# Casting q and k of a pair in one operation, with the tail weights of a spatial product made earlier

## The chip, the cores and the metric

The kernel runs on one core of one Trainium2 chip: TensorE (PE) for matrix products, VectorE (DVE), ScalarE (ACT) and GpSimd (POOL) for the rest, and SyncE (SP), which here only issues DMAs; POOL issues DMAs too. The metric is the device time of one execution in microseconds (us), and lower is better.

## The reference

A gated attention for 8 batches of 8 heads (sequence 576, head dimension 64), whose output goes through a gated MLP with a spatial product over the sequence:

```python
scores = scale * np.matmul(q, k.transpose(0, 1, 3, 2))
cum = np.cumsum(np.maximum(s, 0.0), axis=-1)
bias = -(cum[:, :, :, None] - cum[:, :, None, :])
scores = np.where(causal, -1e9, scores + np.minimum(bias, 0.0))
attn = softmax(scores)
x = (attn @ v) with the heads put side by side        # (8, 576, 512)
h = np.maximum(x @ w_in, 0.0)                          # (8, 576, 1024)
u, v = h[..., :512], h[..., 512:]
v_n = (v - mean(v)) / sqrt(var(v) + 1e-6)
v_s = np.einsum('ts,bsd->btd', w_spatial, v_n) + b_spatial[None, :, None]
return (u * v_s) @ w_out
```

All of it is float32 outside the kernel; w_in and w_out come as float64 and are taken apart bit by bit.

## The kernel before

Products run in float16 with each operand split in two: a high part (the cast to float16) and a low part (the operand less its high part). Attention is done in 32 pairs of heads, p = 0 to 31; the MLP in 8 batches, one for four pairs.

*Scores.* For pairs 3 to 31 (pairs 0 to 2 use float32 operands directly) the scores of a pair are two products added up in PSUM (L300 to 304): QA with KA, and QB with KB, each of 128 rows that are summed over. KA holds in rows 64 to 127 the high part of k and in rows 61 to 63 the prefix sums of s in three parts (`cc`, brought by `aux_rows`, L212, three DMAs); QA holds in rows 64 to 127 the high part of q and in rows 0 to 63 the constant 8 (131360.0 as a float32 is two float16 8.0), so that rows 61 to 63 add 8 times the prefix sums; rows 0 to 60 of KA are zero. Both are set once by POOL (`init_static`, L130). KB and QB carry the cross terms: low k with high q in the lower half, high k with low q in the upper half. There are three buffers of each, used in turn (p % 3).

*How a pair is split.* `load_raw` (L227, POOL's queue) brings k in partitions 0 to 63 and q in partitions 64 to 127 of one float32 tile. `split_raw` (L233) then does k and q one after the other: DVE casts k to a tile kh of 64 partitions, of which there is one buffer; SP sends it to KA and to KB; DVE makes the low part of k. ACT casts q into QA, SP sends it on to QB, and POOL makes the low part of q in four pieces.

*Softmax and the second product.* `s_pass` (L276): DVE adds the mask and takes the row's extreme (L307), ACT takes the exponential (L313), DVE the reciprocal of the sum (L317, L318), ACT and DVE the high and low part of the weights (L322, L323), and SP transposes them with a DMA (L328), two large ones and one for the last 64 rows per pair. `av_pass` (L401 and L408) multiplies with v, whose two parts `fetch_v` and `load_v` (L255, L263) prepare for two pairs at a time.

*MLP.* For each batch: the v half in five tiles of 128 rows, the last one of 64 rows laid on both halves of the partitions (L443, normalised in L459 to L478: POOL makes 1/sqrt(var), L469 and L470, and six DMAs spread the last tile over vx and VY, L482 to 484); then the u half (L494); then the spatial product (L507), which ends with the last 64 rows: L509 takes vx with wx1, and L510 takes VY with wx2, whose rows 0 to 63 are the low part of the tail weights and whose rows 64 to 66 are the bias in three parts; then the output product (L529).

*Order.* PE's order is written by hand: each step has a position on a common axis (`at`, L545), scores of pair p stand at 2p to 2p + 5/3, the second product at 2p + 3.72, the MLP of batch b from 8b + 10.3 on, and PE follows the sorted list. The other engines and the two DMA queues are ordered by a list planner, by position and by when it reckons things to be ready; steps marked `True` go first, and those before position 12.4 that are not so marked follow the last marked one on their engine. An engine runs its list in order, and a DMA that waits holds up what is behind it on its queue.

*Weights.* While the first pairs run, the kernel also brings and splits its weights: w_in (`fetch_win`, `load_win`), w_spatial (`load_wsp`, L190, positions 11 to 12.2), w_out (`load_wout`, L187, 10.6 to 13.9) and the tail with the bias (`load_wtail`, L195, position 13). The first spatial product stands at about 13.9, the first output product at about 16.1.

Of the kernel before, what the change touches and what calls it, by code (L numbers as in the profile page):

```python
# [19 lines left out]
SWSP = 1024.0  # L20
# [10 lines left out]
def attn_gated_mlp(ctx, tc, kqT, v, s, w_in, w_spT, b_sp, w_out, outT):  # L31
    nc = tc.nc
    P = 128
    NHB, D, H, S = kqT.shape
# [95 lines left out]
    def init_static(i):  # L130

        nc.gpsimd.memset(QA[i][0:64].rearrange("p h s -> p (h s)").bitcast(F32), 131360.0)
        nc.gpsimd.memset(KA[i][0:64].rearrange("p h s -> p (h s)").bitcast(F32), 0.0)
        if i < 2:
            nc.gpsimd.memset(VY[i][64:96], 2048.0)
# [59 lines left out]
    def load_wtail():  # L195
# [3 lines left out]
        split_w(wx1, wx2, s4, SWSP, N_W3 > 4)  # L199
        bf = wk.tile([1, S], F32, tag="ob", bufs=2, name="bf")  # L200
        bp = wk.tile([1, 3, S], F16, tag="wst", bufs=1, name="bp")
        nc.sync.dma_start(out=bf, in_=b_sp)
# [5 lines left out]
        for i in range(3):  # L208
            nc.sync.dma_start(out=wx2[TAIL + i:TAIL + i + 1], in_=bp[:, i])
# [13 lines left out]
    def raw_rows(hb, hs, nm):  # L223
        src = kqT[hb, 0:64, hs] if nm == "k" else kqT[hb, 64:128, hs]
        return nc.sync.dma_start(out=raws[hb, hs.start, nm][64:128], in_=src)

    def load_raw(p):  # L227
# [3 lines left out]
        nc.gpsimd.dma_start(out=raws[p], in_=kqT[hb, :, 2 * pr:2 * pr + 2])  # L231

    def split_raw(nm, p):  # L233


        i = p % 3
        raw = raws[p] if nm == "k" else raws.pop(p)
        lo, hi = slice(0, 64), slice(64, 128)
        if nm == "k":
            kh = wk.tile([64, 2, S], F16, tag="kh", bufs=1, name=f"kh{p}")  # L240
            nc.vector.tensor_copy(kh, raw[lo])
            nc.sync.dma_start(out=KA[i][hi], in_=kh)
            nc.sync.dma_start(out=KB[i][hi], in_=kh)
            nc.vector.tensor_tensor(out=KB[i][lo], in0=raw[lo], in1=kh, op=ALU.subtract)
        else:
            nc.scalar.copy(QA[i][hi], raw[hi])  # L246
            nc.sync.dma_start(out=QB[i][lo], in_=QA[i][hi])
            for j in range(2):
                for c in (slice(0, TH), slice(TH, S)):
                    nc.gpsimd.tensor_tensor(out=QB[i][hi, j, c], in0=raw[hi, j, c], in1=QA[i][hi, j, c],  # L250
                                            op=ALU.subtract)
# [319 lines left out]
    at(-18.9, True, native_cum, 1)  # L571
    at(0.5, True, behind, "c", load_raw, 3)
# [3 lines left out]
    at(1.9, True, aux_rows, 3)  # L576
    for nm in "kq":
        at(2.1, True, split_raw, nm, 3)
# [7 lines left out]
    for hb in range(2, NHB):  # L586
        for pr in range(2):
            p = 2 * hb + pr
            at(2 * p - 5.2, False, load_raw, p)
            at(2 * p - 1.2, False, aux_rows, p)  # L590
# [77 lines left out]
```

## Time and profile before

| | |
|---|---|
| median of 3 runs | 743.84 us (746.62, 743.84, 734.99) |
| the profiled execution | 734.97 us |
| its span, first to last instruction | 733.2 us |
| mean granted clock of PE | 0.943 |
| busy, us | PE 600.2, DVE 607.0, ACT 520.9, POOL 226.0 |
| DMA queue of SP (hardware) | 78.74 MB, 57.2% of 16 engines' span |
| DMA queue of POOL (software) | 35.07 MB, 16.5% |

Busy time is the time in which an engine runs instructions; idle time counts only where it ends on what is late, and the profile names the releaser of each wait. PE is the engine that ends the program. "Granted clock" is the share of TensorE's full speed that the throttle allowed. The page cuts the span in 40 slices of 18.3 us; a digit is the busy share in tenths:

```profile

DVE  8889999795879899789979898999789897985531
PEclk9788577995999999999999999999999999999999
DMA  8997747866279597967797698969986979465001
```

### The profile page before, as it was taken

The numbers are of one execution on the slowest core, as the hardware profiler recorded it, in microseconds if no ns is written. First come the engines' busy times: TensorE is split into PE (matmuls) and PEld (weight loads), VectorE is DVE, ScalarE is ACT, GpSimd is POOL, SyncE is SP. The second block draws the span as 40 slices with busy tenths as digits, with TensorE's granted clock in tenths as the row PEclk, the third lists the DMA queues.
The fourth block names the chain that finished last, engine by engine and source line by source line (L and its number), as shares of the span: only waits on it lengthen the run. The fifth ranks groups of instructions, "written<-read, shape, count | busy, mean of one in ns | idle before, by whom it ended". The sixth has DMA issues, their size and how long they took to land. (4 is left out here: it accounts for less than half of the span.)

```text
span 733.2 us, 15915 instructions
## 1 busy us (share of the span) xinstructions
PE 600.2 (82%) x5696; PEld 415.7 (57%) x5696; DVE 607.0 (83%) x1660; ACT 520.9 (71%) x1328; POOL 226.0 (31%) x303
## 2 busy tenths in 40 slices
PE   4474375741998899889989889997999898999997
PEld 2152132531774677466756666565756665777576
DVE  8889999795879899789979898999789897985531
ACT  4787578663678777877877868786788787875322
POOL 9105465451123432342225331432034322100100
PEclk9788577995999999999999999999999999999999
DMA  8997747866279597967797698969986979465001
GB/s 224 289 201 132 199 99 198 171 176 156 56 169 202 131 180 181 209 136 160 177 191 161 159 163 184 211 128 167 206 200 123 178 131 179 99 107 123 32 13 64
DMA packets 235101, 114.81 MB, mean 157 GB/s; under 512 B 213471, under 2 KB 216717, under 8 KB 235022
## 3 DMA queue, kind: packets, MB, share of 16 engines
q1 hardware_dynamic: 225726, 78.74, 57.2%
q0 software_dynamic: 9296, 35.07, 16.5%
q8 instruction: 44, 0.72, 0.4%
q14 instruction: 35, 0.29, 0.1%
HBM read 37.28 MB, written 9.44 MB: 64 GB/s over the span
## 5 line engine op out<-in xcount | busy, mean ns | idle before, releaser
L313 ACT ACTIVATE p<-psS,mx 128x256 f32<-128x256 f32 (+3 forms) x256 | 132.9, 524 | 72.5 <-DVE mx L307 57.9
L250 POOL TENSOR_TENSOR QB<-raw,QA 64x288 f16<-64x288 f32 x116 | 118.4, 1049 | 213.2 <-ACT QA L246 175.9
L307 DVE CUSTOM_DVE_ANT_0 psS<-psS,mb 128x512 f32<-128x512 f32 (+2 forms) x320 | 154.3, 493 | 14.2 <-PE psS L303 12.0
L323 DVE SCALAR_TENSOR_TENSOR pb<-p,sm,pb 128x384 f16<-128x384 f32 (+3 forms) x256 | 134.8, 559 | 2.1 <-ACT pb L322 1.6
L322 ACT ACTIVATE pb<-p,sm 128x384 f16<-128x384 f32 (+3 forms) x256 | 122.8, 555 | 7.0 <-DVE sm L318 3.2
L443 PE MATMUL vps<-win,xt 128*128 128x512 f16 (+1 forms) x576 | 105.2, 354 | 18.6 <-ACT ob L532 9.6
L303 PE MATMUL psS<-KA,QA 128*128 128x128 f16 (+1 forms) x348 | 82.9, 312 | 40.4 <-ACT p L313 37.7
L507 PE MATMUL sps<-ws,vn 128*128 128x288 f16 x768 | 106.7, 289 | 10.8 <-DVE g L512 7.2
L494 PE MATMUL ups<-xt,win 128*128 128x288 f16 x768 | 106.6, 293 | 0.6 <-ACT u L497 0.4
L529 PE MATMUL ops<-g,wo 128*128 128x288 f16 x768 | 101.8, 286 | 1.1 <-DVE g L515 1.0
L507 PEld LDWEIGHTS <-vn 128*128 128x128 f16 x768 | 74.6, 99 | 35.9 <-issue 13.2
L494 PEld LDWEIGHTS <-win 128*128 128x128 f16 x768 | 75.6, 100 | 28.7 <-issue 5.1
L303 PE MATMUL psS<-KB,QB 128*128 128x128 f16 (+1 forms) x348 | 89.3, 306 | 1.1 <-DMA QB<-QA 1.1
L529 PEld LDWEIGHTS <-wo 128*128 128x128 f16 x768 | 74.5, 98 | 24.3 <-issue 2.0
L443 PEld LDWEIGHTS <-xt 128*128 128x128 f16 (+1 forms) x576 | 48.4, 103 | 67.8 <-issue 29.4
L401 PE MATMUL av<-pT,V 128*64 128x128 f16 (+2 forms) x960 | 64.0, 282 | 19.7 <-DMA pT<-pb 19.6
L401 PEld LDWEIGHTS <-V 128*64 128x64 f16 x960 | 52.0, 114 | 37.2 <-issue 26.6
L469 POOL TENSOR_SCALAR rs<-mv 128x1 f32<-128x1 f32 x40 | 12.5, 312 | 134.1 <-DVE mv L467 124.0
L303 PEld LDWEIGHTS <-QA 128*128 128x128 f16 x348 | 30.6, 103 | 39.1 <-issue 29.1
L313 ACT ACTIVATION_READ_ACCUMULATOR p<-psS,mx 128x1 f32 x256 | 51.0, 199 | 0.0
L514 ACT CAST g<-g 128x288 f16<-128x288 f32 x64 | 27.1, 429 | 30.4 <-DVE g L512 29.1
L303 PEld LDWEIGHTS <-QB 128*128 128x128 f16 x348 | 30.2, 103 | 30.1 <-issue 16.3
(121 smaller groups left out, 923.4 us busy)
## 6 DMA issues: line engine op xcount, KB each, us to landing
raw<-in_kqT_dram POOLq DMA_DIRECT2D x29, 576.0 KB, 4.7
out_dram<-ob SPq DMA_DIRECT2D x32, 288.0 KB
vraw<-in_v_dram POOLq DMA_DIRECT2D x16, 512.0 KB, 6.9
KA<-kh SPq DMA_DIRECT2D x29, 144.0 KB
KB<-kh SPq DMA_DIRECT2D x29, 144.0 KB
QB<-QA SPq DMA_DIRECT2D x29, 144.0 KB
wst<-in_w_in_dram POOLq DMA_DIRECT2D x8, 512.0 KB, 7.4
vraw<-in_v_dram POOLq DMA_DIRECT2D x16, 128.0 KB, 6.9
```

Source lines behind the costliest of these rows:

```text
L250: nc.gpsimd.tensor_tensor(out=QB[i][hi, j, c], in0=raw[hi, j, c], in1=QA[i][hi, j, c], op=ALU.subtract)
L303: nc.tensor.matmul(ps[m, c0:c0 + w], U[i][:, g, q0:q0 + n], T[i][:, g, k0:k0 + w], start=st, stop=not st)
L307: nc.vector.tensor_tensor_reduce(out=ps[:, c0:c0 + w], in0=ps[:, c0:c0 + w], in1=mask, op0=ALU.add, op1=ALU.min, scale=-0.125, scalar=3.0e ...
L313: nc.scalar.activation(p32, ps[:, c0:c0 + w], AF.Exp, bias=mx[:, col:col + 1], scale=-1.0, accum_out=sm[:, acc:acc + 1])
L322: nc.scalar.activation(dst[:, off:off + w], p32, AF.Copy, bias=0.0, scale=sm[:, col:col + 1])
L323: nc.vector.scalar_tensor_tensor(out=dst[:, n + off:n + off + w], in0=p32, scalar=sm[:, col:col + 1], in1=dst[:, off:off + w], op0=ALU.mul ...
L401: nc.tensor.matmul(dst, V[i][:, jc, h + j], rhs, start=jc == n == 0 and q0 > 0, stop=jc == 3 and n == 2)
L443: nc.tensor.matmul(ps[m, 0:w], xx[:, c, t * P:t * P + (m.stop - m.start)], ww[:, c, NF + g * w:NF + g * w + w], start=c == n == 0, stop=c ...
L494: nc.tensor.matmul(ps[:, 0:TH], ww[:, c, fs], xx[:, c, ts], start=n == 0, stop=n == 3 * KC - 1)
L507: nc.tensor.matmul(ps[:, 0:TH], vv[:, c, fs], ww[:, c, ts], start=n == 0, stop=False)
L514: nc.scalar.copy(g1[:, f, ts], g32)
L529: nc.tensor.matmul(ps[:, 0:TH], ww[:, f, ms], gg[:, f, ts], start=n == 0, stop=n == 3 * FC - 1)
```

## The change

q now lies in partitions 0 to 63 of the raw tile and k in 64 to 127. `split_raw` does both together: ACT casts all 128 partitions into KA (so KA's lower half holds q, its upper half k); SP copies q's high part from there to the upper half of QA, and k's high part to the lower half of KB; DVE makes both low parts in one subtraction into QB; SP copies k's low part from QB's upper half to KB's upper half, and then overwrites QB's upper half with q's high part; last, `aux_rows` overwrites rows 61 to 63 of KA with the prefix sums. Since KA's rows 0 to 60 now hold q and not zero, QA's rows 0 to 60 are set to zero and only rows 61 to 63 to the constant, by a clear and a select on POOL; KA is no longer cleared. The tile kh and POOL's subtractions are gone.

The bias rows leave `load_wtail` for a step of their own, `load_bias`, at position -18.8 among the first steps, with its DMAs on POOL's queue. The tail weights' split stays on ACT and DVE (it was on DVE already with N_W3 = 5), with the low part made for 64 partitions only, and moves from position 13 to 11.5. The spatial weights move from 11 + 0.4c to 9.9 + 0.4c, the output weights from 10.6 + 1.1c to 12 + 0.8c, the split of a pair from 2p - 1.2 to 2p - 1.9, the fetch of v from 4hb - 0.5 to 4hb + 0.2 and its split from 4hb + 1.5 to 4hb + 1.9.

```diff
     NH = B * H
@@ -129,8 +129,10 @@
 
     def init_static(i):
 
-        nc.gpsimd.memset(QA[i][0:64].rearrange("p h s -> p (h s)").bitcast(F32), 131360.0)
-        nc.gpsimd.memset(KA[i][0:64].rearrange("p h s -> p (h s)").bitcast(F32), 0.0)
+        nc.gpsimd.memset(QA[i][0:64].rearrange("p h s -> p (h s)").bitcast(F32), 0.0)
+        q = QA[i][0:64].rearrange("p h s -> p (h s)").bitcast(F32)
+        nc.gpsimd.affine_select(out=q, in_=q, pattern=[[0, S]], compare_op=ALU.is_ge, fill=131360.0, base=60,
+                                channel_multiplier=-1)
         if i < 2:
             nc.gpsimd.memset(VY[i][64:96], 2048.0)
 
@@ -196,17 +198,21 @@
         s4 = wk.tile([P, S], F32, tag="ob", bufs=2, name="wsx_st")
         nc.sync.dma_start(out=s4[0:TAIL], in_=w_spT[NFULL * P:S])
         nc.sync.dma_start(out=s4[TAIL:2 * TAIL], in_=w_spT[NFULL * P:S])
-        split_w(wx1, wx2, s4, SWSP, N_W3 > 4)
+        nc.scalar.activation(wx1, s4, AF.Copy, bias=0.0, scale=SWSP)
+        nc.vector.scalar_tensor_tensor(out=wx2[0:TAIL], in0=s4[0:TAIL], scalar=SWSP, in1=wx1[0:TAIL], op0=ALU.mult,
+                                       op1=ALU.subtract)
+
+    def load_bias():
         bf = wk.tile([1, S], F32, tag="ob", bufs=2, name="bf")
         bp = wk.tile([1, 3, S], F16, tag="wst", bufs=1, name="bp")
-        nc.sync.dma_start(out=bf, in_=b_sp)
+        nc.gpsimd.dma_start(out=bf, in_=b_sp)
         nc.vector.tensor_scalar(bf, bf, SWSP * SVN / 2048.0, None, op0=ALU.mult)
         for i in range(3):
             nc.vector.tensor_copy(bp[:, i], bf)
             if i < 2:
                 nc.vector.tensor_tensor(out=bf, in0=bf, in1=bp[:, i], op=ALU.subtract)
         for i in range(3):
-            nc.sync.dma_start(out=wx2[TAIL + i:TAIL + i + 1], in_=bp[:, i])
+            nc.gpsimd.dma_start(out=wx2[TAIL + i:TAIL + i + 1], in_=bp[:, i])
 
 
     def aux_rows(p):
@@ -221,34 +227,28 @@
             raws[hb, hs.start, nm] = wk.tile([P, 2, S], F32, tag=tag, bufs=bufs, name=f"{nm}raw{hb}")
 
     def raw_rows(hb, hs, nm):
-        src = kqT[hb, 0:64, hs] if nm == "k" else kqT[hb, 64:128, hs]
+        src = qkT[hb, 0:64, hs] if nm == "q" else qkT[hb, 64:128, hs]
         return nc.sync.dma_start(out=raws[hb, hs.start, nm][64:128], in_=src)
 
     def load_raw(p):
 
         hb, pr = divmod(p, 2)
         raws[p] = wk.tile([P, 2, S], F32, tag="raw", bufs=2, name=f"raw{p}")
-        nc.gpsimd.dma_start(out=raws[p], in_=kqT[hb, :, 2 * pr:2 * pr + 2])
-
-    def split_raw(nm, p):
+        nc.gpsimd.dma_start(out=raws[p], in_=qkT[hb, :, 2 * pr:2 * pr + 2])
+
+    def split_raw(p):
 
 
         i = p % 3
-        raw = raws[p] if nm == "k" else raws.pop(p)
+        raw = raws.pop(p)
         lo, hi = slice(0, 64), slice(64, 128)
-        if nm == "k":
-            kh = wk.tile([64, 2, S], F16, tag="kh", bufs=1, name=f"kh{p}")
-            nc.vector.tensor_copy(kh, raw[lo])
-            nc.sync.dma_start(out=KA[i][hi], in_=kh)
-            nc.sync.dma_start(out=KB[i][hi], in_=kh)
-            nc.vector.tensor_tensor(out=KB[i][lo], in0=raw[lo], in1=kh, op=ALU.subtract)
-        else:
-            nc.scalar.copy(QA[i][hi], raw[hi])
-            nc.sync.dma_start(out=QB[i][lo], in_=QA[i][hi])
-            for j in range(2):
-                for c in (slice(0, TH), slice(TH, S)):
-                    nc.gpsimd.tensor_tensor(out=QB[i][hi, j, c], in0=raw[hi, j, c], in1=QA[i][hi, j, c],
-                                            op=ALU.subtract)
+        nc.scalar.copy(KA[i], raw)
+        nc.sync.dma_start(out=QA[i][hi], in_=KA[i][lo])
+        nc.sync.dma_start(out=KB[i][lo], in_=KA[i][hi])
+        nc.vector.tensor_tensor(out=QB[i], in0=raw, in1=KA[i], op=ALU.subtract)
+        nc.sync.dma_start(out=KB[i][hi], in_=QB[i][hi])
+        nc.sync.dma_start(out=QB[i][hi], in_=KA[i][lo])
+        aux_rows(p)
 
     vraws = {}
 
@@ -569,13 +569,12 @@
     at(-19, True, native_tiles, 1)
     at(-19, True, native_sel, 1)
     at(-18.9, True, native_cum, 1)
+    at(-18.8, True, load_bias)
     at(0.5, True, behind, "c", load_raw, 3)
     at(0.6, True, init_static, 0)
     at(0.6, True, behind, "c", fetch_v, 0)
     at(1.4, True, load_v, 0)
-    at(1.9, True, aux_rows, 3)
-    for nm in "kq":
-        at(2.1, True, split_raw, nm, 3)
+    at(2.1, True, split_raw, 3)
     at(2.1, True, native_tiles, 2)
     at(2.1, True, native_sel, 2)
     at(3, True, native_cum, 2)
@@ -587,19 +586,17 @@
         for pr in range(2):
             p = 2 * hb + pr
             at(2 * p - 5.2, False, load_raw, p)
-            at(2 * p - 1.2, False, aux_rows, p)
-            for nm in "kq":
-                at(2 * p - 1.2, False, split_raw, nm, p)
-        at(4 * hb - 0.5, False, fetch_v, hb)
-        at(4 * hb + 1.5, False, load_v, hb)
+            at(2 * p - 1.9, False, split_raw, p)
+        at(4 * hb + 0.2, False, fetch_v, hb)
+        at(4 * hb + 1.9, False, load_v, hb)
     for c in range(KC):
         at(2.2 + 1.2 * c, False, fetch_win, 1, c)
         at(4.5 + c, False, fetch_win, 0, c)
         at(6.5 + 0.5 * c, False, load_win, 1, c)
         at(9 + 0.5 * c, False, load_win, 0, c)
-        at(11 + 0.4 * c, False, load_wsp, c)
-        at(10.6 + 1.1 * c, False, load_wout, c)
-    at(13, False, load_wtail)
+        at(9.9 + 0.4 * c, False, load_wsp, c)
+        at(12 + 0.8 * c, False, load_wout, c)
+    at(11.5, False, load_wtail)
     for p in range(NP):
         units([2 * p + k / 3 for k in range(6)], p < 4, s_pass, p)
         at_av = 2 * p + 3.72 if p != 3 else 9.4
@@ -643,7 +640,7 @@
 
     B, H, S, D = inputs['q'].shape
     lay = {
-        'kqT': _np.concatenate([inputs[n].reshape(2 * B, H // 2, S, D).transpose(0, 3, 1, 2) for n in 'kq'], axis=1),
+        'qkT': _np.concatenate([inputs[n].reshape(2 * B, H // 2, S, D).transpose(0, 3, 1, 2) for n in 'qk'], axis=1),
         'v': inputs['v'].transpose(0, 2, 1, 3).reshape(B, S, H * D),
         's': inputs['s'].reshape(B * H, S),
         'w_in': inputs['moe_w_in'],
```

More of the change, by code (lines that the diff above doesn't have):

```diff
@@ L30, in attn_gated_mlp @@
 @with_exitstack
-def attn_gated_mlp(ctx, tc, kqT, v, s, w_in, w_spT, b_sp, w_out, outT):
+def attn_gated_mlp(ctx, tc, qkT, v, s, w_in, w_spT, b_sp, w_out, outT):
     nc = tc.nc
     P = 128
-    NHB, D, H, S = kqT.shape
+    NHB, D, H, S = qkT.shape
     B, H, D = NHB // 2, 2 * H, D // 2
```

## The prediction

> **What bounds the kernel now.** I read the windows first (times in us: PE busy, PE weight loads, DVE, ACT, POOL, each with its count; then the granted PE clock and the DMA share).
>
> ```profile
> 0.00:125.00 125.00, 65.03 (x458) 35.63 (x459) 115.10 (x281) 87.14 (x209) 58.46 (x77) 0.81 0.82 193
> 125.00:200.00 75.00, 44.49 (x426) 31.46 (x425) 58.39 (x138) 43.68 (x102) 25.60 (x29) 0.80 0.62 140
> 200.00:650.00 450.00, 411.46 (x4115) 290.00 (x4114) 397.73 (x1149) 357.04 (x936) 137.86 (x188) 1.00 0.83 167
> ```
>
> Up to 125 us DVE is the bound (115.10 of 125, PE only 65.03). From 200 us on PE is (411.46 of 450), with DVE close behind at 397.73, so PE loses 38.5 us there. In between, PE loses 30.5 us and DVE is idle for 16.6 us as well: both wait for something. The timeline of PE (start, duration, work, idle time before it and its releaser) shows what:
>
> ```profile
> 159.04 0.28 PE L507 MATMUL sps<-ws,vn 128*128 128x288 f16 x1 [1.72 <-ACT ws L148]
> 161.27 0.41 PE L507 MATMUL sps<-ws,vn 128*128 128x288 f16 x2 [1.94 <-DVE ws L150]
> 172.32 0.40 PE L509 MATMUL sps<-wx,vx 128*128 128x288 f16 x1 [10.65 <-DMA vx<-tl]
> 180.19 0.40 PE L510 MATMUL sps<-wx,VY 67*128 67x288 f16 x1 [7.46 <-DMA wx<-bp]
> ```
>
> The first spatial product of the first MLP waits in turn for spatial weights (1.72 + 1.94), for the tail rows of the normalised activations (10.65) and for the bias rows (7.46): 21.8 of the 30.5 us, in one place. The waits of PE between 200 and 650 us (who, for whom, total, times, longest) are spread thin:
>
> ```profile
> PE psS L303 <- ACT p L313: 14.6, 11, 2.4
> PE vps L443 <- ACT ob L532: 9.6, 5, 2.5
> PE sps L507 <- DVE g L512: 7.2, 5, 2.3
> PE av L401 <- DMA pT<-pb: 4.5, 2, 2.5
> ```
>
> **The change part by part.** *Bias rows and tail weights.* The DVE rows of the bias (count, min/median/max in ns):
>
> ```profile
> L203 DVE TENSOR_SCALAR bf<-bf x1: 448/448/448, 174.9 to 174.9; 1x576 f32<-1x576 f32 x1
> L205 DVE CAST bp<-bf x3: 448/449/449, 175.4 to 177.9; 1x576 f16<-1x576 f32 x3
> L207 DVE TENSOR_TENSOR bf<-bf,bp x2: 747/747/747, 175.9 to 177.2; 1x576 f32<-1x576 f32 x2
> ```
>
> 0.45 + 3 x 0.45 + 2 x 0.75 = 3.3 us of DVE, with four DMAs, leave 173-180 us for the start. The wait of 7.46 us goes entirely: the cover is some 150 us of other work. The spatial weights come 1.1 positions earlier and the tail 1.5 (scores of a pair take two positions; 64 of them fill about 650 us, so one is some 10 us, an estimate), ahead of the output weights; so 1.72 and 1.94 go too. What is late next is the tail's activations (rows picked from the timelines of DVE, POOL and SP, in the order in which they matter):
>
> ```profile
> 156.05 0.19 DVE L467 BATCH_NORM_AGGREGATE mv<-st 128x2 f32<-128x12 f32 x1
> 155.61 3.99 POOL L250 TENSOR_TENSOR QB<-raw,QA 64x288 f16<-64x288 f32 x4 [1.75 <-issue]
> 159.69 0.24 POOL L469 TENSOR_SCALAR rs<-mv 128x1 f32<-128x1 f32 x1
> 163.62 1.23 DVE L471 TENSOR_SCALAR hv<-hv,mv,rs 128x256 f32<-128x256 f32 x1
> 159.91 4.75 SPq L328 DMA_TRANSPOSE pT<-pb  x1
> 164.76 0.54 SPq L197 DMA_DIRECT2D wsx_st<-in_w_spT_dram  x1
> ...
> 169.17 0.59 SPq L484 DMA_DIRECT2D vx<-tl  x1
> ```
>
> The statistics are ready at 156.2, but POOL is inside the low parts of a q until 159.6, so the scale starts 3.5 us late and everything behind it; on SP the six tail copies stand behind a transpose and two loads of tail weights. The change takes away both the POOL block and the two loads (1.2 us). Best case: 156.2 + about 2.5 for scale, multiply and split, + 3.7 for six copies + 2.1 to land (row below) = 164.5, and the bias product starts then instead of at 180.19: -15.5. Worst: the transpose still stands in front, 164.7 + 3.7 + 2.1 = 170.5: -9.7. I take the middle, -12, which holds the weights' 3.7. PE runs at 0.80 of its clock between 125 and 200 us; a shorter hole should give back some of that: between 0 and -3, I take -1.5.
>
> *Casts and low parts.* Rows of before (min/median/max in ns), and one operation on 128 partitions:
>
> ```profile
> L241 DVE CAST kh<-raw x29: 741/751/1340, 10.2 to 597.0; 64x1152 f16<-64x1152 f32 x29
> L244 DVE TENSOR_TENSOR KB<-raw,kh x29: 1340/1346/2094, 11.7 to 606.5; 64x1152 f16<-64x1152 f32 x29
> L246 ACT CAST QA<-raw x29: 1147/1148/1149, 8.5 to 607.9; 64x1152 f16<-64x1152 f32 x29
> L250 POOL TENSOR_TENSOR QB<-raw,QA x116: 721/736/3909, 11.4 to 611.2; 64x288 f16<-64x288 f32 x116
> L267 DVE SCALAR_TENSOR_TENSOR V<-vraw,V x16: 1470/1479/2021, 18.5 to 615.4; 128x1280 f16<-128x1280 f32 x16
> L241 DVE CAST kh<-raw 64x1152 f16<-64x1152 f32 x8 | 6.8, 852 | 1.0 <-DMA KB<-kh 1.0
> ```
>
> 128 partitions cost what 64 do: 1479 ns for 1280 elements is 1.16 ns each, 1346 for 1152 is 1.17. So ACT's one cast stays at 1.15 us and DVE's one subtraction at 1.35; DVE's 29 casts (24.7 us) and POOL's 116 subtractions go. Eight casts, 6.8 us, lie before 162 us (last row, the groups of that stretch alone), where DVE is the bound; the bias puts 3.3 us back, at the start. POOL also holds DVE up:
>
> ```profile
> 71.53 2.98 DVE L170 SCALAR_TENSOR_TENSOR wt<-wst,wt 128x512 uint32<-128x512 uint32 x1
> 71.84 2.11 POOL L250 TENSOR_TENSOR QB<-raw,QA 64x288 f16<-64x288 f32 x3
> L170 DVE SCALAR_TENSOR_TENSOR wt<-wst,wt x12: 662/674/2981, 38.4 to 185.8; 128x512 uint32<-128x512 uint32 x12
> ```
>
> 2.98 against a median of 0.67 us while POOL subtracts: 2.3 us in this one event. The ramp's best is -6.8 + 3.3 - 2.3 = -5.8; its worst has the 3.3 us on the path to the first scores and nothing else used, +3.3. I take -4, nearer the first, since DVE is 92% busy there. The Trainium skill (SBUF — State Buffer, section "SBUF: two separate sides") says that the port pair which DVE and GpSimd share is an exclusive lock, and the loser blocks for a whole instruction. By that rule at most the 116 x 0.74 = 85 us of POOL's subtractions stop holding DVE up; PE's 38.5 us of idle time after 200 us cap what that is worth there, and the sum would be 711.5 - (38.5 - 6) = 679. Only the one event above bears it out: L244, with two SBUF inputs, has a median of 1346 against a minimum of 1340, so few operations meet the lock, and the case gets under 0.02.
>
> After 200 us, 21 casts (17.9 us by the mean of 852) leave DVE. PE's waits there that go back to DVE are 14.6 + 7.2 = 21.8; DVE's load falls by 17.9 of 397.7, 4.5%. A gain of 1 us (4.5% of 21.8) is one end, 17.9 the other; I take -6, as DVE is second to PE by little.
>
> *The new order of DMAs.* Six copies a pair become seven, and they now depend on each other: k's low part goes out of QB's upper half, which is then overwritten with q, and the three rows of prefix sums overwrite KA only after that copy has read it. Landing and slack, rows picked from the timelines of SP, DVE and PE in the steady part:
>
> ```profile
> 316.09 1.92 SPq L214 DMA_DIRECT2D KA<-cc  x3
> 318.69 0.54 SPq L243 DMA_DIRECT2D KB<-kh  x1
> 321.34 1.20 DVE L241 CAST kh<-raw 64x1152 f16<-64x1152 f32 x1 [0.62 <-DMA KB<-kh]
> 338.32 0.22 PE L303 MATMUL psS<-KA,QA 128*128 128x128 f16 x1
> 329.76 1.37 SPq L328 DMA_TRANSPOSE pT('t', 13)_3791<-pb  x1
> 335.99 0.67 PE L408 MATMUL avt<-pT('t', 13)_3791,V 128*64 128x64 f16 x30
> 342.41 4.80 SPq L328 DMA_TRANSPOSE pT<-pb  x1
> ```
>
> A copy issued by 319.23 releases the next cast at 321.34: 2.1 us to land. The chain after the change is 1.15 + 1.35 + two times (0.54 + 2.1) + 1.92 + 2.1 = 11.8 us; the rows of before went out at 316 for scores at 338.32, 22 us earlier, and the step is planned 0.7 positions sooner. So the chain itself is hidden in the steady part: 0. In the ramp there is less room, hence the positive end there. On SP it costs 0.54 of issue and up to two landings, 4.2, in which SP stands still: 4.7 a pair. What queues behind is a transpose, as at 342.41; a tail transpose issued at 329.76 lands at 329.76 + 1.37 + 2.1 = 333.2 for a use at 335.99, slack 2.8. If the list puts other ready work into the gaps the price is 0; if never, 4.7 - 2.8 = 1.9 a pair. I take 0 and keep the other end as a rival. The Trainium skill (DMA: Bandwidth & Descriptors, section "Anatomy of one DMA — SWDGE (gpsimd) path") speaks against the change: DMA engines do not wait on semaphores, the issuing sequencer does. With its 2.0 us fixed cost, an estimate by that page is 4.5 a pair in place of 4.7, and the rival's price hardly moves.
>
> *The rest.* POOL loses three clears of KA and gets three selects; by L250's 0.72 us for 288 elements a select of 576 is under 1.5 us, on an engine that is half idle: 0. Bias DMAs on POOL hold its queue while DVE makes the rows, at most 3.3 us, inside the ramp's positive end. V's fetch and split move by 0.7 and 0.4 positions, the output weights by up to 1.4 later, still 1.7 positions before their first use: 0. The matrix products are the same in number and shape.
>
> Sum: -12 - 1.5 - 4 - 6 = -23.5. The profiled execution took 734.97 us (span 733.2), so 711.5. The three timed runs lie at 734.99, 743.84 and 746.62: the profile stands at their low end, 8.9 below the median. I put the median of after half of that above the sum: 716.
>
> **The rivals.** (1) *SP becomes the bound.* Waiting copies in front of the transposes, 1.9 us a pair for about 25 pairs, +48: 716 + 48 = 764, slower. It decides as soon as half of the pairs pay, since 24 us use up the gain. For it: SP's large transposes above take 4.75 and 4.80 us each, and copies and transposes stand in one queue. Against it: the list is made by readiness, and PE waited only 4.5 us for transposes in 450 us.
> (2) *The hole moves, DVE fills it.* Positions are only priorities, so the tail might not come sooner; and DVE needs 58.39 of the 75 us between 125 and 200, with two output weights pushed into that stretch. Then only the bias wait (7.46) and 4.5 us of the other terms count, 735.0 - 12 + 4.4 = 727.5, about 2% below the median.
> (3) *Late operands in the ramp.* Two more landings and a copy, 4.7 us, in front of pairs 4 to 7, +19: 735, within 2%. PE did wait for KA's copy once before, with the old, shorter chain:
>
> ```profile
> 72.22 0.22 PE L303 MATMUL psS<-KA,QA 128*128 128x128 f16 x1 [2.71 <-DMA KA<-kh]
> ```
>
> Against it: DVE has work of the weights to do in such holes, and DVE is the bound there.
>
> **How the numbers follow.** Forecast (700 to 729 by the ends of its terms) 0.57, the lock's case within it; rival 2 0.20; rival 3 0.09; rival 1 0.14. A measurement of this kernel can tell about 2% from no change, so faster means below 729: nearly all of the forecast and a quarter of rival 2, 0.61; slower is above 759, rival 1 with a weak form that stays below: 0.13; the rest 0.26. The range reaches from 700 to 742: it leaves out rival 1 and little at the bottom.
>
> **What would show it.** Right: no bias wait before the first product with VY; that product 10 to 15 us sooner; no POOL subtractions; DVE at about 582 us busy (607.0 - 24.7); PE's waits for transposes as before. Wrong: SP idle in front of copies of QB or prefix sums with transposes behind them, waits of PE for pT or KA over 20 us in total, or first scores more than 3 us later.

## The result, and the profile after

The changed kernel takes 755.77 us (median of 4 runs, 752.82 to 759.16) against 744.24 us before; the ratio is 1.0301, with a 95% interval of 1.0236 to 1.0367. It is slower by 3%, outside the predicted range and on the other side of the forecast. (Here and below the ratios leave disturbed runs out and the medians do not, so the two don't divide exactly.) The profiled execution took 756.74 us, 21.8 more than that of before.

The windows of the changed kernel (columns as in the prediction) say where the time went. For the stretch from 200 us on, one row of the kernel before with the same bounds follows.

```profile
0.00:125.00 125.00, 60.07 (x454) 34.54 (x456) 106.23 (x278) 84.22 (x205) 36.22 (x62) 0.81 0.90 202
125.00:200.00 75.00, 55.05 (x514) 39.58 (x514) 59.73 (x165) 52.67 (x132) 13.68 (x20) 0.86 0.72 153
200.00:675.00 475.00, 419.99 (x4055) 295.72 (x4053) 368.84 (x1106) 349.67 (x913) 53.16 (x99) 0.96 0.77 163
```

```profile
200.00:675.00 475.00, 436.29 (x4358) 309.06 (x4358) 415.86 (x1205) 372.30 (x978) 137.86 (x188) 1.00 0.82 163
```

PE does nearly the same list of products in both kernels, so its counts show how far each has come. By 200 us the changed kernel is ahead: 454 + 514 = 968 products against 458 + 426 = 884. From 200 to 675 us it does 303 fewer (4055 against 4358). At before's pace there (475 us for 4358, so 0.109 us each) the 84 are worth 9.2 us and the 303 cost 33.0: together 23.8 us lost, about the 21.8 that the two executions differ by. So the start did gain, and the steady part lost more than three times as much, though DVE and POOL both have less to do in it. The same two rows split the 33.0 us: PE is idle for longer (475 - 419.99 = 55.0 us, against 36.0 for as many products at before's rate), 19.0 us; and a product takes longer (419.99 us for 4055, 103.6 ns, against 100.1), 14.0 us, at a granted clock of 0.96 where it was 1.00. The count of products between 200 and 675 us is used below as the measure of the steady part.

The gain is the hole in the first spatial product. The timeline of PE shows the bias product 11.2 us earlier than at 180.19, with no wait in front of it and none for the tail's activations:

```profile
168.90 0.29 PE L509 MATMUL sps<-wx,vx 128*128 128x288 f16 x1
169.02 0.29 PE L510 MATMUL sps<-wx,VY 67*128 67x288 f16 x1
```

The loss shows in the waits (who, for whom: us in total, times, longest), first those of the engines, then those of SP's queue:

```profile
DVE QB L248 <- ACT KA L245: 50.9, 10, 9.7
PE av L401 <- DMA pT<-pb: 50.8, 17, 7.8
ACT ob L532 <- DMA out_dram<-ob: 44.9, 12, 8.1
PE psS L303 <- DMA KA<-cc: 9.2, 1, 9.2
```

```profile
SPq L250 <- DMA KB<-QB: 82.1, 23, 8.0
SPq L220 <- DMA QB<-KA: 56.9, 28, 5.8
```

In the kernel before, the whole-span waits for transposes and for outputs were smaller:

```profile
PE av L401 <- DMA pT<-pb: 19.6, 7, 4.2
ACT ob L532 <- DMA out_dram<-ob: 12.6, 9, 4.0
```

From 200 to 675 us alone PE's wait for transposes at L401 is 30.4 us, against 4.5 in the kernel before.

SP now stands for 82.1 + 56.9 = 139 us, 4.8 us for each of the 29 pairs, in front of a copy that overwrites what another copy is still reading. The timeline of SP for one pair shows what stands behind:

```profile
448.83 0.60 SPq L246 DMA_DIRECT2D QA<-KA  x1
449.52 0.54 SPq L247 DMA_DIRECT2D KB<-KA  x1
450.11 0.60 SPq L249 DMA_DIRECT2D KB<-QB  x1
453.01 0.46 SPq L250 DMA_DIRECT2D QB<-KA  x1
455.32 1.30 SPq L220 DMA_DIRECT2D KA<-cc  x2
456.72 3.07 SPq L328 DMA_TRANSPOSE pT<-pb  x1
459.88 1.36 SPq L328 DMA_TRANSPOSE pT('t', 19)_5529<-pb  x1
461.30 1.16 SPq L534 DMA_DIRECT2D out_dram<-ob  x2
```

From 448.83 to 456.72 nothing leaves but the copies of the split: SP stands 2.3 us of that at L250 (450.71 to 453.01) and 1.9 at the prefix rows (453.47 to 455.32). The transpose goes out at 456.72 and the outputs at 461.30. What that transpose turns was complete at 448.93, so it goes out 7.8 us late; the last row of DVE that writes it:

```profile
448.45 0.48 DVE L323 SCALAR_TENSOR_TENSOR pb<-p,sm,pb 128x256 f16<-128x256 f32 x1
```

Read in this way, the large transposes between 200 and 675 us go out 4.1 us after their last row at L323 in the mean; in the kernel before it is 0.5 us. The timelines of PE, ACT and DVE show what the lateness starts:

```profile
461.87 2.35 PE L401 MATMUL av<-pT,V 128*64 128x384 f16 x27 [4.20 <-DMA pT<-pb]
464.49 0.41 ACT L532 ACTIVATE ob<-ops 128x288 f32<-128x288 f32 x1 [8.52 <-PE av L401]
466.45 0.41 ACT L532 ACTIVATE ob<-ops 128x288 f32<-128x288 f32 x1 [1.55 <-DMA out_dram<-ob]
467.42 1.15 ACT L245 CAST KA<-raw 128x1152 f16<-128x1152 f32 x1
468.60 1.36 DVE L248 TENSOR_TENSOR QB<-raw,KA 128x1152 f16<-128x1152 f32 x1 [9.74 <-ACT KA L245]
```

PE waits 4.20 us for the transpose, and then its granted clock is halved for a while:

```profile
462.70:466.10 3.40, 3.40 (x53) 2.86 (x49) 0.00 (x0) 0.41 (x1) 0.00 (x0) 0.50 1.04 215
```

Whether the wait brings the lower clock was not tested. ACT, in order, stands for 8.52 and 1.55 us, both times until an output tile has been written out. (The row of the 8.52 us names PE's second product, which ended at the same time; but L532 reads a product of L529, done by 454.7 us, and there are two output tiles, both full until the outputs that left at 461.30 have landed.) Only then comes ACT's cast of the next pair, and DVE, in order too, has stood for 9.74 us in front of the subtraction that needs the cast. One block of copies on SP reaches PE by the transpose, and ACT and DVE by the outputs.

### The profile page after: what moved, and what is told of

Its sections match the earlier page's. It is cut to its first block, busy times and chain, and to the rows that moved or that the text cites. A ratio compares the mean times of both kernels' runs of the same rounds, so it can differ in the third digit from the quotient of the medians.

```text
span 755.0 us, 15813 instructions
## 1 busy us (share of the span) xinstructions
PE 611.2 (81%) x5696; PEld 426.1 (56%) x5696; DVE 567.5 (75%) x1631; ACT 518.5 (69%) x1328; POOL 107.1 (14%) x191
## 5 line engine op out<-in xcount | busy, mean ns | idle before, releaser
L313 ACT ACTIVATE p<-psS,mx 128x512 f32<-128x512 f32 (+3 forms) x256 | 133.3, 525 | 55.6 <-DVE mx L307 54.2
L307 DVE CUSTOM_DVE_ANT_0 psS<-psS,mb 128x512 f32<-128x512 f32 (+3 forms) x320 | 155.6, 498 | 15.2 <-PE psS L303 12.7
L323 DVE SCALAR_TENSOR_TENSOR pb<-p,sm,pb 128x384 f16<-128x384 f32 (+3 forms) x256 | 132.2, 552 | 7.5 <-ACT pb L322 7.3
L322 ACT ACTIVATE pb<-p,sm 128x384 f16<-128x384 f32 (+3 forms) x256 | 122.9, 557 | 15.7 <-DMA pT<-pb 7.4
L401 PE MATMUL av<-pT,V 128*64 128x128 f16 (+2 forms) x960 | 76.5, 309 | 51.0 <-DMA pT<-pb 50.8
L443 PE MATMUL vps<-win,xt 128*128 128x512 f16 (+1 forms) x576 | 102.2, 348 | 8.5 <-ACT ob L532 6.8
L529 PE MATMUL ops<-g,wo 128*128 128x288 f16 x768 | 103.1, 289 | 0.2 <-DVE g L515 0.2
L494 PEld LDWEIGHTS <-win 128*128 128x128 f16 x768 | 75.7, 100 | 45.4 <-issue 15.5
L401 PEld LDWEIGHTS <-V 128*64 128x64 f16 x960 | 61.1, 124 | 71.2 <-issue 61.1
L529 PEld LDWEIGHTS <-wo 128*128 128x128 f16 x768 | 75.2, 99 | 23.7 <-issue 0.4
L443 PEld LDWEIGHTS <-xt 128*128 128x128 f16 (+1 forms) x576 | 47.9, 103 | 55.3 <-issue 15.5
L248 DVE TENSOR_TENSOR QB<-raw,KA 128x1152 f16<-128x1152 f32 x29 | 39.2, 1353 | 50.9 <-ACT KA L245 50.9
L532 ACT ACTIVATE ob<-ops 128x288 f32<-128x288 f32 x64 | 25.5, 416 | 70.0 <-DMA out_dram<-ob 44.9
L237 POOL DMA_DIRECT2D raw<-in_qkT_dram x29 | 16.9, 582 | 251.0 <-DVE sm L369 100.2
L313 ACT ACTIVATION_READ_ACCUMULATOR p<-psS,mx 128x1 f32 x256 | 50.9, 199 | 0.0
L307 DVE DVE_READ_ACCUMULATOR2_ANT mx<- 128x1 f32 x320 | 45.1, 141 | 0.0
```

The costliest lines, as they stand in the source:

```text
L248: nc.vector.tensor_tensor(out=QB[i], in0=raw, in1=KA[i], op=ALU.subtract)
L307: nc.vector.tensor_tensor_reduce(out=ps[:, c0:c0 + w], in0=ps[:, c0:c0 + w], in1=mask, op0=ALU.add, op1=ALU.min, scale=-0.125, scalar=3.0e ...
L313: nc.scalar.activation(p32, ps[:, c0:c0 + w], AF.Exp, bias=mx[:, col:col + 1], scale=-1.0, accum_out=sm[:, acc:acc + 1])
L322: nc.scalar.activation(dst[:, off:off + w], p32, AF.Copy, bias=0.0, scale=sm[:, col:col + 1])
L323: nc.vector.scalar_tensor_tensor(out=dst[:, n + off:n + off + w], in0=p32, scalar=sm[:, col:col + 1], in1=dst[:, off:off + w], op0=ALU.mul ...
L401: nc.tensor.matmul(dst, V[i][:, jc, h + j], rhs, start=jc == n == 0 and q0 > 0, stop=jc == 3 and n == 2)
```

## The experiments

Theory S: the copies that wait for other copies, in SP's in-order queue, hold up what stands behind them. The rivals: R, one more copy of 144 KB per pair loads the DMA engines; D, VectorE's place in order behind the cast; P, the moved bias and weight steps. Each ratio is against the kernel before on the same chip; the runs were spread over four chips, so medians of different rows compare less well than ratios. The table has them in the order of the text; "SP stands" is the sum of SP's waits for the landing of copies of the split, "PE for pT" PE's wait at L401 in the whole span, with that from 200 to 675 us behind it in brackets, and "products" the count of PE's products from 200 to 675 us, all from the one profiled execution (that of x7 took 735.55 us, above its median).

| run | median us | ratio (95%) | SP stands | PE for pT | products |
|---|---|---|---|---|---|
| before | 744.24 | 1 | 0 | 19.6 (4.5) | 4358 |
| changed | 755.77 | 1.030 (1.024 to 1.037) | 139.0 | 50.8 (30.4) | 4055 |
| x3, split alone | 767.50 | 1.033 (1.024 to 1.041) | 124.0 | 50.9 (26.7) | 4115 |
| x2, moves alone | 733.32 | 0.987 (0.979 to 0.994) | 0 | 18.7 (6.1) | 4380 |
| x1, two steps on POOL | 739.84 | 0.996 (0.990 to 1.001) | 0 | 15.5 (0.3) | 4419 |
| x12, rows on POOL | 743.56 | 1.012 (1.006 to 1.018) | 110.1 | 29.4 (9.0) | 4130 |
| x6, later positions | 760.94 | 1.026 (1.019 to 1.033) | 141.3 | 40.9 (29.0) | 4052 |
| x4, before + chained | 757.05 | 1.026 (1.018 to 1.035) | 99.4 | 17.4 (4.5) | 4166 |
| x5, before + unchained | 741.64 | 1.005 (0.999 to 1.010) | 0 | 23.7 (11.2) | 4320 |
| x10, scratch tile | 731.65 | 0.984 (0.977 to 0.992) | 83.7 | 25.7 (8.1) | 4340 |
| x9, one standing | 718.40 | 0.973 (0.965 to 0.981) | 93.6 | 10.8 (0.2) | 4443 |
| x7, no standing on SP | 726.86 | 0.981 (0.971 to 0.991) | 0 | 25.6 (9.1) | 4299 |
| x11, outputs on POOL | 751.61 | 1.015 (1.003 to 1.027) | 140.0 | 58.8 (43.0) | 4209 |
| x8, q's low part on POOL | 737.59 | 0.992 (0.986 to 0.997) | 67.7 | 10.5 (0.7) | 4387 |

**The two halves of the change.** x3 is the kernel before with the new split and its row layout alone (`...` stands for lines that are as in the change):

```diff
...
-            at(2 * p - 1.2, False, aux_rows, p)
-            for nm in "kq":
-                at(2 * p - 1.2, False, split_raw, nm, p)
+            at(2 * p - 1.9, False, split_raw, p)
...
```

> The kernel before with the new split alone (one 128-partition cast, one VectorE subtraction, four copies and three prefix rows on SP, place 2p-1.9, new row layout); bias rows, weights and v at their old places. Theory S and rival R: the loss of the split without the gain of the closed hole, 762 to 772 us, SP's waits at L250 and L220 together over 120 us. Rival P (the position moves are what costs): 735 to 745 us.

It took 767.50 us, and SP stood 75.0 us at QB <- KA and 49.0 us at the prefix rows. Part of its loss falls before 200 us: 456 + 311 = 767 products by then, against 884 before. x2 is the complement, the changed kernel with before's split:

```diff
...
-            at(2 * p - 1.9, False, split_raw, p)
+            at(2 * p - 1.2, False, aux_rows, p)
+            for nm in "kq":
+                at(2 * p - 1.2, False, split_raw, nm, p)
...
```

> The changed kernel with the split of before put back (separate q and k casts, VectorE and POOL low parts, old row layout, old place 2p-1.2): so the bias rows made first, the tail weights at 11.5, the weight casts and the two v steps at their new places, alone. Theory S and rival R: the hole of 11 us in the first spatial products is closed and nothing is lost elsewhere, so about 730 to 735 us. Rival P (the moved bias and weight steps cost as much in the start as the hole gave): 740 to 750 us, with the first product of values later than 32.7 us.

It took 733.32 us: the moves gain 1.3%, the split costs 3.3%, and the two make 2.0% where the change measured 3.0%, within what the intervals allow. Rival P falls as the cause of the loss. One part of it was seen: the first large second product starts at 43.37 us in x2, at 37.99 in x3 and at 37.38 before, so the moves, of which the bias steps come first, cost about 6 us there, less than the hole returns.

**Taking the waiting steps off SP.** x1 issues the last copy and the prefix rows from POOL's queue:

```diff
-            nc.sync.dma_start(out=KA[p % 3][61 + r:62 + r], in_=cc[2 * p:2 * p + 2, r])
+            nc.gpsimd.dma_start(out=KA[p % 3][61 + r:62 + r], in_=cc[2 * p:2 * p + 2, r])
...
-        nc.sync.dma_start(out=QB[i][hi], in_=KA[i][lo])
+        nc.gpsimd.dma_start(out=QB[i][hi], in_=KA[i][lo])
```

> The changed kernel, with the copy QB <- KA and the three prefix-row transfers of each pair (L250, L220) issued from POOL's queue instead of SP's; same transfers, same bytes, same order of casts. Theory S (copies that wait for another copy's landing stand in SP's in-order queue and hold the transposes and output transfers behind them): SP's wait at L220 (56.9 us) goes, that at L250 (82.1 us) becomes a wait of POOL's queue, PE's wait for pT falls from 50.8 us towards the 19.6 us of before, and the time falls to 715 to 735 us. Rival R (one more 144 KB copy per pair loads the DMA engines, whichever queue issues it): still 750 to 760 us and PE's wait for pT stays near 50 us. Rival D (the VectorE subtraction stands in order behind ScalarE's cast, L248 <- L245 50.9 us): that wait stays near 50 us and the time stays above 745 us.

The waits of x1:

```profile
POOL QB L250 <- DMA KB<-QB: 108.2, 19, 12.8
POOL KA L220 <- DMA QB<-KA: 62.5, 23, 4.9
ACT ob L532 <- DMA out_dram<-ob: 22.1, 11, 4.1
DVE QB L248 <- ACT KA L245: 18.4, 7, 4.5
PE av L401 <- DMA pT<-pb: 15.5, 4, 8.9
```

The same standing, 170.7 us of it, now lies on POOL's queue, which has less on it that is urgent. PE's wait for transposes falls from 50.8 to 15.5, ACT's for outputs from 44.9 to 22.1 and DVE's for the cast from 50.9 to 18.4; the steady part goes from 4055 products to 4419. The large transposes go out 0.4 us after their last row at L323, against 4.1 in the changed kernel. The time, 739.84, is 16 us below the changed kernel and 5 above the range given, so S holds and is not all; R and D, which both foresaw no gain, fall for this step.

x12 leaves QB <- KA on SP and moves the rows alone (the first of the two edits of x1):

> The changed kernel with the three prefix-row transfers of each pair (L220) on POOL's queue, and QB <- KA left on SP: so SP still stands until KB <- QB has landed (82.1 us in the changed kernel), but no longer until QB <- KA has landed (56.9 us). If the first standing, which begins only after VectorE's subtraction, carries the loss, as the fast version that keeps only the second one suggests: 748 to 757 us, PE's wait for pT above 35 us. If the two add up, each by its length: about 749 to 750 us by 56.9 of 139 us of the 16 us that the POOL-queue version won, with PE's wait for pT near 35 us. If the second standing carries it: 738 to 744 us and PE's wait for pT near 16 us.

The median, 743.56 us, lies in the range of the third reading. By the ratios, which allow for the chip, it lies between (1.030, 1.012, 0.996): moving the rows wins about half of what x1 won, nearest the second reading, with PE's wait for transposes at 29.4 where that reading had near 35 and the third near 16. It doesn't follow that each standing costs half wherever it stands: x9, below, keeps the second and loses nothing. SP stood longer at the one that was left (110.1 us against 82.1) and the time fell all the same, so the sum of SP's standing is not by itself a price.

x6 tried to give SP something else to do in between, by three steps: the cast, the first two copies and the subtraction; then KB <- QB (`split_kb`); then QB <- KA with the prefix rows (`split_qb`); the positions:

```diff
...
-            at(2 * p - 1.9, False, split_raw, p)
+            at(2 * p - 2.4, False, split_raw, p)
+            at(2 * p - 1.7, False, split_kb, p)
+            at(2 * p - 0.9, False, split_qb, p)
...
```

> The changed kernel with the same transfers on the same queue, but each copy that reads what another operation or copy has first to finish in a step of its own: cast, first two copies and subtraction at 2p-2.4, KB <- QB at 2p-1.7, QB <- KA and the prefix rows at 2p-0.9. Theory S: SP no longer stands at these copies (waits at the two lines together under 50 us, against 139), PE's wait for pT falls below 30 us and the time to 715 to 735 us. Rival R (bytes): 750 to 760 us. If the scheduler's list ignores the positions, the order on SP stays and the time with it; that would tell nothing between them.

SP stood 81.6 + 59.7 us, as before that edit, and the time was 760.94 us. For 21 of the 29 pairs the list put QB <- KA right behind KB <- QB again, as many as in the changed kernel; this run doesn't tell the theories apart, but it shows that a position does not keep a waiting copy away from the copy that it waits for.

**Chains against bytes.** x4 and x5 add two copies of 74 KB per pair to the kernel before, into a tile that nobody reads. They differ only in what the copies read. In x4 each reads what the copy before it writes (the first follows QB <- QA):

```diff
+    scr = cp.tile([P, S], F16, name="scr")
...
+            nc.sync.dma_start(out=scr[lo], in_=QB[i][lo, 0])
+            nc.sync.dma_start(out=scr[hi], in_=scr[lo])
```

In x5 both read what ScalarE has cast:

```diff
...
+            nc.sync.dma_start(out=scr[lo], in_=QA[i][hi, 0])
+            nc.sync.dma_start(out=scr[hi], in_=QA[i][hi, 0])
```

> The kernel before with two more copies of 74 KB per pair on SP's queue, into a scratch tile that nobody reads: the first reads QB, which a copy issued just before it has to fill, the second reads what the first has filled. So SP stands at two landings per pair and the DMA engines carry 148 KB more. Theory S: about 750 to 765 us, as the standing of the changed kernel (139 us on SP) costs; PE's wait for pT above 35 us (19.6 before). Rival R (bytes): the same time as the twin with unchained copies, within 5 us.

> The kernel before with the same two more copies of 74 KB per pair on SP's queue and the same scratch tile, but both read QA, which ScalarE has written: no copy waits for the landing of another. Theory S: within 5 us of the kernel before (740 to 748 us); PE's wait for pT stays near 20 us. Rival R (bytes): as slow as the chained twin, 750 us or more.

757.05 against 741.64 us. The page gives both the same transfers on SP's queue (queue: packets, MB, share of 16 engines), first x4, then x5:

```profile
q1 hardware_dynamic: 230366, 83.02, 56.4%
```

```profile
q1 hardware_dynamic: 230366, 83.02, 59.0%
```

The same 83.02 MB cost nothing that can be measured in x5 and 2.6% in x4, where SP's waits are

```profile
SPq L254 <- DMA QB<-QA: 54.9, 18, 5.9
SPq L255 <- DMA scr<-QB: 44.5, 18, 5.8
```

Rival R falls for one extra copy. One reading of S was wrong: PE's wait for transposes did not rise in x4 (17.4). What the standing held up was other things: ACT's wait for outputs to land rose to 20.8 us (11.2 in x5), and DVE's cast waited 23.9 us for its one kh tile to be sent (14.9 in x5). From 200 to 675 us PE's waits that name ACT come to 35.2 us in x4 and 23.7 in x5, which is where part of the 15 us reached PE; how the rest did isn't settled. In x4 a copy reads what another writes; in the changed kernel a copy overwrites what another reads. SP stands for a landing in both.

**Without the chain, with the work kept.** x10 keeps the one VectorE subtraction, into a scratch tile of its own, so that no copy waits for another; only the prefix rows still do:

```diff
-        nc.vector.tensor_tensor(out=QB[i], in0=raw, in1=KA[i], op=ALU.subtract)
-        nc.sync.dma_start(out=KB[i][hi], in_=QB[i][hi])
         nc.sync.dma_start(out=QB[i][hi], in_=KA[i][lo])
+        nc.vector.tensor_tensor(out=lw, in0=raw, in1=KA[i], op=ALU.subtract)
+        nc.sync.dma_start(out=KB[i][hi], in_=lw[hi])
+        nc.sync.dma_start(out=QB[i][lo], in_=lw[lo])
```

> The changed kernel with its one VectorE subtraction kept, but written to a scratch tile of its own, from which both low parts are copied; QB <- KA then waits for the cast alone. So five copies of 144 KB per pair (one more than the changed kernel, two more than before), and SP stands only ahead of the prefix rows. Theory S, as the runs so far bear it out (the copy that waits for another copy costs, one standing per pair does not): 712 to 728 us, PE's wait for pT under 22 us. Rival R (bytes and number of copies): no better than the changed kernel, 750 us or more. Rival L (it was the landing of the low part that came late for the scores, since it went through a copy): near 740 us with scores waiting for KB or QB.

731.65 us, 24 below the changed kernel and 4 above the range given (PE's wait for transposes, 25.7 us, is above the 22 given too), with more bytes than any other run:

```profile
q1 hardware_dynamic: 230268, 87.29, 60.2%
```

R falls by this run too, and so does L: no wait of PE's names KB or QB.

x9 needs neither tile nor copy: VectorE writes the low parts in two operations of 64 partitions, each where it belongs, and KB <- QB falls away; SP stands once per pair, in front of the prefix rows. x7 is x9 with those rows on POOL's queue.

```diff
-        nc.vector.tensor_tensor(out=QB[i], in0=raw, in1=KA[i], op=ALU.subtract)
-        nc.sync.dma_start(out=KB[i][hi], in_=QB[i][hi])
         nc.sync.dma_start(out=QB[i][hi], in_=KA[i][lo])
+        nc.vector.tensor_tensor(out=KB[i][hi], in0=raw[hi], in1=KA[i][hi], op=ALU.subtract)
+        nc.vector.tensor_tensor(out=QB[i][lo], in0=raw[lo], in1=KA[i][lo], op=ALU.subtract)
```

> The changed kernel without either chain: the low parts in two VectorE operations of 64 partitions (k's low part written straight into KB, q's into QB, so the copy KB <- QB falls away), QB <- KA waits for the cast alone, and the prefix rows come from POOL's queue. VectorE gets one more operation of about 1.35 us per pair (39 us in all, back to the 607 us of before). Theory S: SP's waits for landings are gone, PE's wait for pT under 22 us, 715 to 732 us, faster than the first POOL-queue version, whose POOL stood 108 us for the copy. Rival D (VectorE time and its waits for the cast decide): 740 us or more.

> As the version without a chain, but with the prefix rows left on SP's queue, behind the landing of QB <- KA: one of the two standings per pair is taken away, one (56.9 us in the changed kernel) stays. Theory S: between the changed kernel (756 us) and the version without a chain, 728 to 745 us, with PE's wait for pT between the two. Rival (only the standing at QB <- KA, the longer one, matters): the same as without a chain, within 4 us.

x7 took 726.86 us, in the range given; PE's wait for transposes, 25.6 us, was above the 22 given. x9 took 718.40 us, 2.7% below the kernel before and the fastest of all. Neither of its two readings held: it lies below the range of the first and over 8 us from x7. SP's standing at the rows and PE's wait in x9:

```profile
SPq L220 <- DMA QB<-KA: 89.7, 27, 8.0
```

```profile
PE av L401 <- DMA pT<-pb: 10.8, 4, 5.1
```

A standing of 3.3 us (89.7 / 27) once per pair costs nothing that these runs show, where 4.8 us in two pieces cost the changed kernel 3%. The traces differ in what stands ready behind it: the large transposes go out 0.7 us after their last row at L323 in x9, and 4.1 in the changed kernel. The timeline of SP in x9 shows one pair:

```profile
458.77 0.54 SPq L246 DMA_DIRECT2D QA<-KA  x1
459.41 0.55 SPq L247 DMA_DIRECT2D KB<-KA  x1
460.01 0.59 SPq L248 DMA_DIRECT2D QB<-KA  x1
462.49 1.91 SPq L220 DMA_DIRECT2D KA<-cc  x3
465.01 0.53 SPq L465 DMA_DIRECT2D st<-st  x1
```

The block of copies ends after 5.6 us (458.77 to 464.40), and other work follows. SP stood 1.9 us here. The runs do not show whether the rows do better on SP (x9) than on POOL's queue (x7): the intervals of the two overlap.

**Outputs.** x11 takes the output transfers off SP and leaves both standings:

```diff
-                    nc.sync.dma_start(out=outT[b, ms], in_=ob)
+                    nc.gpsimd.dma_start(out=outT[b, ms], in_=ob)
```

> The changed kernel with the output transfers (L534) issued from POOL's queue; all else, both standings too, as it is. Theory S has two parts: transposes that come late (PE waits for pT 50.8 us) and outputs that come late (ScalarE waits for an output to land 44.9 us, VectorE then for the cast 50.9 us). If the outputs carry a good part: ScalarE's wait for outputs falls to 15 us or less and the time to 740 to 748 us. If the transposes carry it: PE's wait for pT stays near 50 us and the time stays at 750 to 758 us.

ACT's wait for outputs fell to 8.9 us, but PE's for transposes stayed (58.8), and DVE now waited 52.5 us for ACT's part of the second product's output, which waited for PE. The median lies in the second of the two ranges given, and the ratio (1.015) halfway between the changed kernel and before: so late outputs seem to carry a part (the interval, 1.003 to 1.027, touches that of the changed kernel), and with them gone the late transposes reach DVE by another way.

**POOL's pieces.** x8 is x9 with q's low part made by POOL in four pieces, as in the kernel before:

```diff
-        nc.vector.tensor_tensor(out=QB[i][lo], in0=raw[lo], in1=KA[i][lo], op=ALU.subtract)
+        for j in range(2):
+            for c in (slice(0, TH), slice(TH, S)):
+                nc.gpsimd.tensor_tensor(out=QB[i][lo, j, c], in0=raw[lo, j, c], in1=KA[i][lo, j, c], op=ALU.subtract)
```

> The version with one standing (718 us) with q's low part made by POOL in four pieces, as in the kernel before, instead of VectorE. VectorE is freed of 39 us (601 to about 562 us of busy time). If VectorE's time still bounds the steady part: 705 to 713 us. If POOL's pieces come late (they wait for ScalarE's cast in order with POOL's other work, and the raw loads stand behind them) or PE is the bound there: 715 to 728 us.

It was slower than either reading, 737.59 us. VectorE lost 29 operations of 1.348 us, 39.1 us, and its busy time did not fall: 601.1 us in x9, 603.7 in x8. Groups of DVE rows (mean in ns after the comma), first of x9, then of x8 (two lines further down in its code):

```profile
L249 DVE TENSOR_TENSOR KB<-raw,KA 64x1152 f16<-64x1152 f32 x29 | 39.3, 1356 | 10.8 <-ACT KA L245 10.1
L250 DVE TENSOR_TENSOR QB<-raw,KA 64x1152 f16<-64x1152 f32 x29 | 39.1, 1348 | 0.5
L317 DVE TENSOR_SCALAR sm<-sm 128x4 f32<-128x4 f32 (+1 forms) x96 | 16.3, 171 | 2.5 <-ACT p L313 2.1
L366 DVE TENSOR_TENSOR mx<-mx 128x1 f32<-128x1 f32 x32 | 4.8, 151 | 0.4
```

```profile
L249 DVE TENSOR_TENSOR KB<-raw,KA 64x1152 f16<-64x1152 f32 x29 | 44.3, 1532 | 22.2 <-ACT KA L245 21.7
L319 DVE TENSOR_SCALAR sm<-sm 128x4 f32<-128x4 f32 (+1 forms) x96 | 23.2, 244 | 10.2 <-ACT p L315 9.1
L368 DVE TENSOR_TENSOR mx<-mx 128x1 f32<-128x1 f32 x32 | 13.5, 421 | 0.8
```

The same operations take 1532 against 1356 ns, 244 against 171 and 421 against 151 in the mean when POOL subtracts.

## Why the prediction was wrong

*The hole.* Right in mechanism and size: -12 was put on it, the bias product came 11.2 us sooner (169.02), and no wait for weights, tail or bias is left. (Its best case is 164.5 - 180.19 = -15.7, not -15.5; that changes nothing.) The clock between 125 and 200 us rose from 0.80 to 0.86, as the small term for it said. x2, the moves alone, is the one run that shows this gain by itself: 1.3%, about 10 us.

*The new order of DMAs.* This is the step that failed: "If the list puts other ready work into the gaps the price is 0; if never, 4.7 - 2.8 = 1.9 a pair. I take 0 and keep the other end as a rival". The list put other transfers between KB <- QB and QB <- KA for 8 of the 29 pairs, and between QB <- KA and the rows for 12: SP stood 4.8 us a pair, and the steady part lost 33.0 us, 1.6 for each of the 21 pairs split there, close to the end that was set aside. That the size comes so near is in part luck. The slack of 2.8 us was read from a transpose of the last 64 rows, and PE's 50.8 us of waiting are at L401, for the large ones, which go out 4.1 us late; and of the 33.0 us, 14.0 are products that take longer at the lower granted clock, which the sum had no term for in the steady part. The argument for 0, that the list is made by readiness and that PE waited only 4.5 us for transposes, was one about the kernel before, in which no copy of a pair waited for another; it could not tell what the list does with copies that do. x6 shows that for most pairs the list packs them together even when their positions are apart. Rival 1 was thus the mechanism, and its condition, that half of the pairs pay, was met: SP stood at the rows in 28 of 29 pairs. Its price, +48, was too high by about half; its chance, 0.14, rested on the argument for 0.

*The landing time.* 2.1 us was read from one copy. The standings at L250 average 82.1 / 23 = 3.6 us and reach 8.0. The Trainium skill (DMA: Bandwidth & Descriptors, section "Anatomy of one DMA — SWDGE (gpsimd) path") gives about 2 us of fixed cost for a DMA on POOL's path; the copies here are on SP's queue. The rows are above that figure, at a DMA share of 0.77, so an estimate by that page would have mis-sized this step just as the one row did.

*"The chain itself is hidden in the steady part: 0."* The scores do not wait for KA or QB there, so this was right for its place. But the chain's engines were not looked at: DVE's subtraction stands in order behind ACT's cast, ACT behind the outputs, and DVE waits 50.9 us for the cast. That wait follows the late outputs and so SP's standing: it falls to 18.4 in x1 and to 10.1 in x9 with the same dependence in place.

*The ramp.* -4 was wrong in sign for its first part: the first large second product starts at 45.86 us, 8.5 later than before, of which the moves make about 6 (x2), and pair 4 waited 9.2 us for its prefix rows at 87.10, which is rival 3 in weak form. By 125 us little of it was left: 454 products against 458.

*The steady part's DVE time.* DVE's busy time fell more than foreseen, to 567.5 us and not 582, since POOL's subtractions had lengthened more of DVE's work than the one event that the text went by (607.0 - 24.7 for the casts - 567.5 leaves 14.8 us). Whether the 6 us were there is hidden in this kernel by the standing; x9, without the chain, reaches 718 us, near the 716 of the forecast, but with VectorE at 601 us, so that less VectorE time can't be its reason.

## What to carry to other kernels

A copy that reads what another copy has just written, or overwrites what another still reads, makes its queue stand until that one has landed, and what is ready behind it on that in-order queue pays; so count, for each queue, not the transfers alone but the waits between them, price them at the landing under load, and look at what will be ready behind each. Break the chain first (write the result where it belongs, or to a tile of its own), and only then move it to a queue that has nothing urgent: here a further copy per pair cost less than the wait that it took away (x10). A slack found in the old order of a queue says nothing on what a planner will do with transfers that depend on each other.

## What was not expected of the hardware

POOL's elementwise work can lengthen VectorE's to the point that handing it an operation frees nothing: 39.1 us moved off VectorE in x8, and its busy time went from 601.1 to 603.7 us. The size isn't fixed: 116 subtractions of the same shape had cost VectorE some 14.8 us in the kernel before. The Trainium skill (SBUF — State Buffer, section "SBUF: two separate sides") describes the port pair that the two share as an exclusive lock; x8 goes the same way, with 41.7 us of lengthening (603.7 - 601.1 + 39.1) for 116 POOL operations, though it can't tell a lock from a port that is shared by turns; the prediction had given that rule next to no weight.

The time to land for 144 KB from SBUF to SBUF is not a constant. The DMA issues of x12 (median from issue to landing in the last column):

```profile
KB<-KA SPq DMA_DIRECT2D x29, 144.0 KB, 3.7
KB<-QB SPq DMA_DIRECT2D x29, 144.0 KB, 5.3
QB<-KA SPq DMA_DIRECT2D x29, 144.0 KB, 2.5
```

KB <- QB leaves right behind two copies of the same pair and takes 5.3 us; QB <- KA leaves after the standing, when that copy has landed, and takes 2.5. That the copies ahead make the difference is the likely reading, not one that a run isolates.
